# Attention ahead of a mixture of experts: all products of the exponentials with V in float32, in halves of 64 query columns

## The chip, the core and the metric

The kernel runs on one core of a Trainium2 chip. The metric is the time of one execution on the device, in microseconds (us). The core's engines work on their own queues, each in order, and wait for each other by semaphores: TensorE (PE in the profile, its weight loads PEld), VectorE (DVE), ScalarE (ACT), GpSimd (POOL) and SyncE (SP), which here issues DMAs, as ScalarE does.

## The reference

```python
def attention(q, k, v, g_q, g_k):            # 8 batches, 12 heads, 448 positions, 64 wide, float32
    q_n = q / sqrt(mean(q * q) + 1e-6) * g_q
    k_n = k / sqrt(mean(k * k) + 1e-6) * g_k
    scores = q_n @ k_n.T / sqrt(64)
    attn = exp(scores - max(scores))
    attn = attn / (sum(attn) + 1e-9)
    return attn @ v

x = attention(...)                           # 3584 tokens x 768
logits = x @ w_gate                          # 8 experts
# pairs (token, expert) in falling order of logits: a token goes to an expert if it has none
# yet and the expert has fewer than 448
out[mask_e] = maximum(x[mask_e] @ w1[e], 0) @ w2[e]
```

## The kernel before

The first part, the class `Attention`, takes about 470 us; `Router` and `Experts` take the rest. Attention works on 24 groups of four heads, two pairs of heads in a group. The 448 keys of two neighbouring heads make seven units of 128 keys: three full ones of the first head, unit 3 with 64 keys of either, and three of the second. The steps of a group:

- q and k are loaded, squared (ScalarE), summed (VectorE), scaled by their norms and g (GpSimd), split into a high and a low float16 half (ScalarE high, GpSimd low) and transposed by DMA. A first round of products gives row maxima (`max_score` on TensorE, `max_reduce` on VectorE), which go into q's operand as one more row.
- `scores` (lines 553 and 548) writes the scores of two units into PSUM (ring `psc`), keys in the partitions, and `exp` (line 564) makes of them one float32 tile `e`, 128 x 896, on ScalarE. A group has seven such tiles, d = 0 to 6, each of two units.
- `av` (lines 589 to 617) multiplies the exponentials, as the stationary operand, with V, 64 columns and a column of ones for the sum. For each pair of heads there are seven tasks w. Tasks 0 to 2 and 4 to 6 are whole blocks of 128 query columns of one head; each adds up four key units. Task 3 takes the last 64 columns of the first head into PSUM partitions 0 to 63 and the first 64 of the second into 64 to 127, and issues the two in turn.
- `x_norm`, `x_hi` and `x_lo` (lines 619 to 653) divide by the sums and split the result into float16 halves.

A product with V takes one of two forms, by the tile d. In a *wide* tile (`WIDE`) e is multiplied in float32 by a scaled float32 copy of V, `v32` (line 599). In any other tile the product is split (lines 604, 606 and 608): the upper 16 bits of e, read in place as bfloat16 (`ph`), times the high half of V; the same times V's low half; and the rest `pl` = e - `ph` in float16 times the high half. `split` (line 580) makes `pl` on GpSimd for the tiles of `LO_POOL` and on VectorE for the others. `v_hi` (line 477) and `v_lo` (line 481) make V's halves `vs` on ScalarE and VectorE, `v_full` (lines 486 and 488) makes `v32` on ScalarE. `MIX` gives each group its form: the first three groups have five wide tiles of seven ("5"), the next eighteen have four ("4": 0, 2, 4 and 6), the last three none ("0").

`plan` lists the tasks with their queue, a cost and what they depend on, and `ORDER` is a table of numbers that sets the order in which all tasks are issued. Each engine executes its own in that order. The table of the last batches ends with the router's first steps.

```python
if self.wide(d):
    nc.tensor.matmul(out, self.T["e", d][:, i, q0:q0 + m], self.v32[...], start=first, stop=last)
    continue
h, l = self.T["ph", d], self.T["pl", d]
nc.tensor.matmul(out, h[:, i, q0:q0 + m], vh, start=first, stop=False)
nc.tensor.matmul(out[:, :64], h[:, i, q0:q0 + m], vl[:, :64], start=False, stop=False)
nc.tensor.matmul(out, l[:, i, q0:q0 + m], vh, start=False, stop=last)
```

Of the kernel before, what the change touches and what calls it, by code (L numbers as in the profile page):

```python
# [89 lines left out]
class Attention:  # L90
# [21 lines left out]
    WIDE = {"5": (0, 2, 4, 6, 3), "4": (0, 2, 4, 6), "3": (0, 2, 4), "p": (0, 2, 4), "2": (2, 4), "0": ()}  # L112
    LO_POOL = {"5": (1, 5), "4": (1, 3, 5), "3": (1, 3, 5), "p": (1, 3, 5, 6), "2": (1, 3, 5), "0": (1, 3, 5)}
    MIX = "555" + 18 * "4" + "000"

    def __init__(self, ctx, tc, q, k, v, g_q, g_k, w_gate, xd, logits, router):
# [53 lines left out]
        def values(i):  # L170
            t, r = self.vs[i], self.vraw[i]
            G.memset(t[:, 0, :, 64:65], 1.0)
            for s in range(2):
                h = slice(64 - 64 * s, 128 - 64 * s)
                G.memset(t[h, 0, 2 * s + 1:8:4, 64:65], 0.0)
                G.memset(r[h, 4 * s + 3::8], 0.0)
            G.memset(self.v32[i][:, :, :, 64:65], 1.0)
# [22 lines left out]
        self.pl = {}  # L200
# [249 lines left out]
    def slot(self, a, u, s):  # L450

        w = self.block(a, u) % 4
        return 8 * (w < 2) + 2 * (2 * a + s) + w % 2
# [5 lines left out]
    def quads(self, t, n):  # L459
        return t.rearrange("p (x y) d -> p x y d", y=4)[:, :, 2 * n:2 * n + 2]  # L460

    def narrow(self, g):

        n = [d // 2 for d in (0, 2, 4, 6) if d not in self.by_group(self.WIDE, g)]
        return slice(n[0], n[-1] + 1, max(1, n[-1] - n[0]) if len(n) == 2 else 1) if n else None

    def halves_v(self, g):

        r, vs = self.vraw[g % 2], self.vs[g % 2].rearrange("p j (n x y) d -> p j n x y d", n=2, y=2)
        yield self.quads(r, 1), vs[:, 0, 0, :, :, :64], vs[:, 1, 0, :, :, :64]  # L470
        x = self.narrow(g)
        if x:
            yield self.quads(r, 0)[:, x], vs[:, 0, 1, x, :, :64], vs[:, 1, 1, x, :, :64]

    def v_hi(self, g):
        for r, h, l in self.halves_v(g):
            self.nc.scalar.activation(h, r, AF.Copy, scale=self.VS)

    def v_lo(self, g):
        for r, h, l in self.halves_v(g):  # L480
            self.nc.vector.scalar_tensor_tensor(l, r, self.VS, h, op0=OP.mult, op1=OP.subtract)
# [78 lines left out]
    def exp(self, d):  # L560
# [4 lines left out]
        self.T["ph", d] = e.bitcast(BF).rearrange("p i (c h) -> p i c h", h=2)[:, :, :, 1]  # L565

    def by_group(self, what, g):
        return what[self.MIX[g]]

    def pooled(self, d):  # L570
        g, n = divmod(d, 7)
        return n in self.by_group(self.LO_POOL, g)

    def wide(self, d):
        return d % 7 in self.by_group(self.WIDE, d // 7)

    def split(self, d):
# [5 lines left out]
    def av(self, n):  # L583
# [1428 lines left out]
```

## Time and profile before

| | |
|---|---|
| median of 3 runs | 964.99 us (964.6 to 966.69) |
| the profiled execution | 969.8 us |
| its span, first to last instruction | 968.0 us |
| TensorE busy | 908.1 us (94%), 9212 matmuls |
| VectorE, ScalarE, GpSimd busy | 666.8, 468.8, 437.8 us |
| attention's last products with V | 467 us |

The span is read in stretches: the first 50 us are a start in which TensorE is often without work, from 50 to about 400 the groups follow each other evenly, from 400 to 470 the last groups end without new loads, and behind 470 stand the router and the experts. A matmul's row has a modelled end, and rows overlap; what a matmul costs is read from the start of one to the start of the next. A row "x8" is eight instructions of one kind in a row, and its start is that of the first. A form such as 128*64 says how many rows and columns of the array a matmul uses.

### The profile page before, as it was taken

The numbers are of one execution on the slowest core, as the hardware profiler recorded it, in microseconds if no ns is written. First come the engines' busy times: TensorE is split into PE (matmuls) and PEld (weight loads), VectorE is DVE, ScalarE is ACT, GpSimd is POOL, SyncE is SP. The second block draws the span as 40 slices with busy tenths as digits, with TensorE's granted clock in tenths as the row PEclk, the third lists the DMA queues.
The fourth block names the chain that finished last, engine by engine and source line by source line (L and its number), as shares of the span: only waits on it lengthen the run. The fifth ranks groups of instructions, "written<-read, shape, count | busy, mean of one in ns | idle before, by whom it ended". The sixth has DMA issues, their size and how long they took to land.

```text
span 968.0 us, 22733 instructions
## 1 busy us (share of the span) xinstructions
PE 908.1 (94%) x9212; PEld 583.0 (60%) x9212; DVE 666.8 (69%) x1507; ACT 468.8 (48%) x732; POOL 437.8 (45%) x430
## 2 busy tenths in 40 slices
PE   2899999998999999999779999999999999999996
PEld 1467766666776667676655655556555565655553
DVE  6788896877678767998789777776775858234110
ACT  4867766665775756656324343434342414233110
POOL 7799989778798868853210202111202011120001
PEclk9899999999999989999789999999999999999999
DMA  6397999979999998976163938576766739482101
GB/s 166 100 171 172 197 206 184 205 199 201 219 207 206 188 214 176 172 173 129 60 208 119 265 136 252 181 233 192 216 185 214 202 131 309 156 189 105 34 17 41
DMA packets 278817, 167.76 MB, mean 173 GB/s; under 512 B 198806, under 2 KB 265878, under 8 KB 277688
## 3 DMA queue, kind: packets, MB, share of 16 engines
q1 hardware_dynamic: 254168, 139.43, 60.1%
q0 software_dynamic: 4704, 22.10, 7.0%
q10 hardware_dynamic: 19840, 4.79, 2.6%
q8 instruction: 72, 1.18, 0.5%
q14 instruction: 33, 0.27, 0.1%
HBM read 94.49 MB, written 22.02 MB: 120 GB/s over the span
## 4 chain that ended last, share of the span: by engine, by line
issue 33%; PE 7%; POOL 5%; DVE 2%; DMA 2%; SPq 1%; ACT 0%; POOLq 0%; DVEq 0%
PE ph L1775 6%; POOL rows L1708 2%; POOL out_dram L1811 2%; PE py L1792 1%; DMA stage<-in_moe_w_dram 1%; SPq L1713 1%; DMA xd<-xm 0%; PE rp L1350 0%; DMA rows<-xd,idx 0%; POOL spacer L1810 0%; DVE or L1325 0%; DVE cmp L1335 0%; DVE w1l L1695 0%; PE rp L1421 0%; ACT w2h L1691 0%
## 5 line engine op out<-in xcount | busy, mean ns | idle before, releaser
L1775 PE MATMUL ph<-xt,w1h 128*128 128x448 f16 (+2 forms) x804 | 209.7, 344 | 0.0
L564 ACT ACTIVATE e<-psc 128x896 f32<-128x896 f32 x168 | 152.3, 916 | 94.1 <-PE psc L553 53.3
L599 PE MATMUL po<-v,e 128*128 128x65 f32 (+1 forms) x1392 | 183.2, 269 | 0.6 <-DVE q L412 0.3
L599 PEld LDWEIGHTS po<-v,e 128*128 128x128 f32 (+1 forms) x1392 | 154.5, 179 | 22.3 <-issue 17.1
L1811 POOL DMA_INDIRECT out_dram<-y,idx x32 | 32.7, 1020 | 288.6 <-ACT y L1794 254.7
L580 POOL TENSOR_TENSOR pl<-e 128x896 f16<-128x896 f32 x69 | 118.1, 1713 | 65.9 <-ACT e L564 50.6
L553 PE MATMUL psc<-q,k 128*128 128x448 f16 x576 | 138.1, 361 | 9.6 <-ACT e L564 5.6
L1775 PE MATMUL ph<-xt,w1l 128*128 128x448 f16 (+2 forms) x402 | 135.1, 344 | 0.0
L530 DVE TENSOR_REDUCE mx<-pm 128x2 f32<-128x896 f32 x96 | 104.0, 1084 | 32.2 <-PE pm L519 28.8
L1792 PE MATMUL py<-w2h,hl 128*128 128x384 f16 x384 | 125.0, 326 | 0.0
L1792 PE MATMUL py<-w2h,hh 128*128 128x384 f16 x384 | 125.0, 326 | 0.0
L1792 PE MATMUL py<-w2l,hh 128*128 128x384 f16 x384 | 125.0, 326 | 0.0
L1775 PEld LDWEIGHTS <-w1h 128*128 128x128 f16 x804 | 74.0, 97 | 63.5 <-issue 1.9
L604 PE MATMUL po<-vs,e 128*128 128x65 f16 (+1 forms) x840 | 110.3, 196 | 0.4 <-DVE xm L653 0.4
L606 PE MATMUL po<-vs,e 128*128 128x64 f16 (+1 forms) x840 | 110.0, 194 | 0.0
L608 PE MATMUL po<-vs,pl 128*128 128x65 f16 (+1 forms) x840 | 109.3, 194 | 0.1
L1763 ACT ACTIVATE hh<-ph 128x448 f16<-128x448 f32 x64 | 34.8, 544 | 144.2 <-PE ph L1775 142.5
L1792 PEld LDWEIGHTS <-hh 128*128 128x128 f16 x768 | 73.2, 97 | 46.7
L604 PEld LDWEIGHTS <-e 128*128 128x128 bf16 (+1 forms) x840 | 87.3, 118 | 15.5 <-issue 9.6
L1765 DVE SCALAR_TENSOR_TENSOR hl<-ph,hh 128x448 f16<-128x448 f32 x64 | 39.4, 619 | 72.9 <-ACT hh L1763 72.9
L1708 POOL DMA_INDIRECT rows<-xd,idx x32 | 32.2, 1005 | 123.7 <-PE rp L1543 65.5
L1794 ACT ACTIVATE y<-py 128x384 f32<-128x384 f32 x48 | 23.6, 491 | 129.8 <-PE py L1792 97.0
(292 smaller groups left out, 1811.7 us busy)
## 6 DMA issues: line engine op xcount, KB each, us to landing
stage<-in_moe_w_dram SPq DMA_DIRECT2D x64, 768.0 KB
vraw<-in_v_dram SPq DMA_DIRECT2D x24, 384.0 KB
xd<-xb SPq DMA_DIRECT2D x8, 1152.0 KB
qkraw<-in_q_dram SPq DMA_DIRECT2D x23, 384.0 KB
qkraw<-in_k_dram SPq DMA_DIRECT2D x23, 384.0 KB
k<-k SPq DMA_DIRECT2D x44, 112.0 KB
q<-q SPq DMA_DIRECT2D x44, 112.0 KB
xd<-xm SPq DMA_DIRECT2D x16, 96.0 KB
```

What stands on the lines that cost most here:

```text
L530: self.nc.vector.tensor_reduce(m, p[:, :k, :448], axis=AX.X, op=OP.max)
L553: nc.tensor.matmul(p[:, i, :448], kt[:, a, n:n + 128], qt[:, a, 448 * s:448 * s + 448], start=st, stop=not st)
L564: self.nc.scalar.activation(e, p[:, :, :448], AF.Exp, scale=scale)
L580: eng.tensor_tensor(l, self.T["e", d], self.T["ph", d], op=OP.subtract)
L599: nc.tensor.matmul(out, self.T["e", d][:, i, q0:q0 + m], self.v32[g % 2][:, self.by_group(self.WIDE, g).index(d % 7), i, :], start=first, ...
L604: nc.tensor.matmul(out, h[:, i, q0:q0 + m], vh, start=first, stop=False)
L606: nc.tensor.matmul(out[:, :64], h[:, i, q0:q0 + m], vl[:, :64], start=False, stop=False)
L608: nc.tensor.matmul(out, l[:, i, q0:q0 + m], vh, start=False, stop=last)
L1708: nc.gpsimd.indirect_dma_start(out=g[:n, c, :], out_offset=None, in_=self.xd, in_offset=bass.IndirectOffsetOnAxis(ap=idx[:n, c:c + 1], axi ...
L1775: nc.tensor.matmul(p, a[:, i, c], x[:, b, o], start=j == 0, stop=j == 17)
L1792: nc.tensor.matmul(p, a[:, f, s], b[:, f, o], start=st, stop=sp)
L1811: st = nc.gpsimd.indirect_dma_start(out=self.out, out_offset=bass.IndirectOffsetOnAxis(ap=self.router.idx[k][:n, c:c + 1], axis=0), in_=y[ ...
```

## The change

All tiles are treated as wide, in all groups. The split products, `pl`, `vs`, `v_hi`, `v_lo` and `MIX` are gone. `v_full` makes one scaled float32 copy `v1` of a whole group's V on GpSimd, in one instruction. `av` treats each whole block as task 3 was treated: as two parts of 64 query columns, the first into PSUM partitions 0 to 63 and the second into 64 to 127, and issues them in turn.

```diff
-        self.vs = tiles(2, [128, 2, 16, 65], F16, "vs")
-        self.v32 = tiles(2, [128, max(map(len, self.WIDE.values())), 2, 65], F32, "v32")
+        self.v1 = tiles(2, [128, 16, 65], F32, "v1")
...
     def v_full(self, g):
-        r, o, wide = self.vraw[g % 2], self.v32[g % 2], [d for d in self.by_group(self.WIDE, g) if d != 3]
-        x = slice(wide[0] // 2, wide[-1] // 2 + 1)
-        self.nc.scalar.activation(o[:, :len(wide), :, :64], self.quads(r, 0)[:, x], AF.Copy, scale=self.VS)
-        if 3 in self.by_group(self.WIDE, g):
-            self.nc.scalar.activation(o[:, 4, :, :64], r[:, 6:14:4], AF.Copy, scale=self.VS)
+        self.nc.gpsimd.tensor_scalar(self.v1[g % 2][:, :, :64], self.vraw[g % 2], self.VS, None, op0=OP.mult)
...
-    def split(self, d):
-        l = self.T["pl", d] = self.w.tile([128, 2, 448], F16, name="pl", bufs=self.RINGS["pl"])
-        eng = self.nc.gpsimd if self.pooled(d) else self.nc.vector
-        eng.tensor_tensor(l, self.T["e", d], self.T["ph", d], op=OP.subtract)
...
-                if self.wide(d):
-                    nc.tensor.matmul(out, self.T["e", d][:, i, q0:q0 + m],
-                                     self.v32[g % 2][:, self.by_group(self.WIDE, g).index(d % 7), i, :], start=first, stop=last)
...
+                nc.tensor.matmul(out, self.T["e", d][:, i, q0:q0 + m], self.v1[g % 2][:, self.slot(a, u, s)],
+                                 start=u == us[0], stop=u == us[-1])
...
         if w == 3:
             parts = [part(po[:64, w], 0, 384, 64), part(po[64:, w], 1, 0, 64)]
-        elif w < 3:
-            parts = [part(po[:, w], 0, 128 * w, 128)]
         else:
-            parts = [part(po[:, w], 1, 64 + 128 * (w - 4), 128)]
+            s, q = (0, 128 * w) if w < 3 else (1, 64 + 128 * (w - 4))
+            parts = [part(po[64 * n:64 * n + 64, w], s, q + 64 * n, 64) for n in range(2)]
...
-            put("vhi", "A", "vhi", self.v_hi, g, after=[("v", g), *once("v", g)], make=("vh", g), opens=[("V", g)],
+            put("vfull", "P", "values", self.v_full, g, after=[("v", g), *once("v", g)], make=("V", g), opens=[("V", g)],
                 uses=[("vraw", g)])
...
     ORDER = (
-        "0o02060v0-0w030z000x050+09010A0410080B070y12141t130C151v0D0p0s1611170t181u1Q190u1S1A1R1w1T1x1P1G1U1y1V1H1B1q"
+        "0o02060v0-0w030z000x050+09010A0410080B070y12141r130C151t0D0p0s1611170t181s1Q190u1S1A1R1u1T1v1P1G1U1w1V1H1B1o"
```

The numbers in the new table are other ones since there are fewer tasks; the 2133 tasks that both kernels have stand in the same order in both.

On TensorE, in the middle of attention (group 11), a run of products with V between scores (L553, now L517) and maxima (L519, now L483). Before, from the end of a tile's scores on:

```order
L553 LDWEIGHTS k_3017
L553 MATMUL psc<-q_3065,k_3017 128x448
L553 LDWEIGHTS k_2_127
L553 MATMUL psc<-q_1_129,k_2_127 128x448
L604 LDWEIGHTS e
L604 MATMUL po<-vs_134,e 128x65
L606 LDWEIGHTS e
L606 MATMUL po<-vs_134,e 128x64
L608 LDWEIGHTS pl
L608 MATMUL po<-vs_134,pl 128x65
L599 MATMUL po<-v_0_138,e 128x65 x2
```

Now, at the same place:

```order
L517 LDWEIGHTS k_2856
L517 MATMUL psc<-q_2904,k_2856 128x448
L517 LDWEIGHTS k_2_127
L517 MATMUL psc<-q_1_129,k_2_127 128x448
L542 MATMUL po<-v_0_136,e 64x65 x32
L542 MATMUL po<-v_1_137,e 64x65 x8
L483 LDWEIGHTS q_3493
L483 MATMUL pm<-k_1_126,q_3493 128x448
```

The alternation of float16 and float32 products on 128 columns has become five blocks of eight float32 products on 64 columns; they now stand between products that use the full array and products that use half its rows.

On GpSimd, where V of group 10 is made (the operand v_0_136). Before, between the scaling of another group's k and q and the next group's square roots:

```order
L317 TENSOR_TENSOR kn<-qkraw,st 128x896
L342 TENSOR_TENSOR qn<-qn,gg 128x896
L580 TENSOR_TENSOR pl<-e 128x896 x2
L379 TENSOR_TENSOR ks_3421<-kn,ks_3421 128x2x7x64
L295 TENSOR_TENSOR st<-st 128x28
```

Now, at the same place:

```order
L310 TENSOR_TENSOR kn<-qkraw,st 128x896
L335 TENSOR_TENSOR qn<-qn,gg 128x896
L452 TENSOR_SCALAR v_0_136<-vraw_132 128x16x64
L372 TENSOR_TENSOR ks_3235<-kn,ks_3235 128x2x7x64
L288 TENSOR_TENSOR st<-st 128x28
```

The two differences are gone, and the copy of V stands there, at the place in the table that ScalarE's copy had.

## Rows read from the trace of the kernel before

**Rows 1.** Busy time of each engine in stretches of the span: start and end, length, busy us and instructions of TensorE, its weight loads, VectorE, ScalarE and GpSimd, the granted TensorE clock as a share of 2.4 GHz, the DMA engines' mean share, GB/s.

```profile
50.00:100.00 50.00, 47.99 (x543) 34.05 (x543) 42.60 (x64) 35.33 (x59) 46.25 (x40) 1.00 0.88 181
50.00:400.00 350.00, 334.06 (x4195) 241.16 (x4196) 275.71 (x428) 234.26 (x397) 294.69 (x241) 0.99 0.94 196
250.00:300.00 50.00, 49.15 (x632) 35.84 (x631) 38.37 (x59) 33.34 (x54) 44.29 (x40) 1.00 1.01 205
```

**Rows 2.** Who the matmuls waited for from 50 to 400 us: us in total, times, longest us.

```profile
PE psc L553 <- ACT e L564: 4.5, 4, 1.6
PE psc L553 <- DMA q<-mt: 3.7, 5, 2.1
PE pm L519 <- DMA k<-k: 2.7, 4, 1.2
PE po L712 <- DMA xt<-xb: 1.7, 1, 1.7
```

**Rows 3.** TensorE in order of time, a run of whole blocks in a group "4": start us, length us, engine, line, operation, tiles, form, count.

```profile
246.71 0.64 PE L599 MATMUL po<-v,e 128*128 128x65 f32 x4
247.18 0.19 PE L604 MATMUL po<-vs,e 128*128 128x65 f16 x1
...
247.36 0.64 PE L599 MATMUL po<-v,e 128*128 128x65 f32 x4
...
248.02 0.63 PE L599 MATMUL po<-v,e 128*128 128x65 f32 x4
```

**Rows 4.** TensorE in order of time, the start of two middle blocks.

```profile
112.27 0.40 PE L599 MATMUL po<-v,e 128*64 128x65 f32 x8
112.50 0.20 PE L604 MATMUL po<-vs,e 128*64 128x65 f16 x2
...
232.33 0.40 PE L599 MATMUL po<-v,e 128*64 128x65 f32 x8
232.57 0.20 PE L604 MATMUL po<-vs,e 128*64 128x65 f16 x2
```

**Rows 5.** Groups of TensorE's instructions with V by form: count, busy us, mean ns of one, idle before.

```profile
L599 PE MATMUL po<-v,e 128*128 128x65 f32 x1044 | 164.0, 282 | 0.6 <-DVE q L412 0.3 <-DVE xm L653 0.2
...
L604 PE MATMUL po<-vs,e 128*128 128x65 f16 x630 | 92.1, 195 | 0.4 <-DVE xm L653 0.4
```

**Rows 6.** TensorE in order of time, passages between forms: a product on 128*128, maxima on 64*128, scores on 128*128, a product on 128*128.

```profile
253.01 0.19 PE L608 MATMUL po<-vs,pl 128*128 128x65 f16 x1
253.13 0.36 PE L519 MATMUL pm<-k,q 64*128 64x448 f16 x2
253.33 0.35 PE L519 MATMUL psc<-k,q 64*128 64x448 f16 x2
253.62 0.93 PE L553 MATMUL psc<-q,k 128*128 128x448 f16 x4
254.38 0.56 PE L599 MATMUL po<-v,e 128*128 128x65 f32 x4
```

**Rows 7.** TensorE in order of time, a middle block behind maxima.

```profile
363.85 0.35 PE L519 MATMUL psc<-k,q 64*128 64x448 f16 x2
364.13 0.45 PE L599 MATMUL po<-v,e 128*64 128x65 f32 x8
364.41 0.20 PE L604 MATMUL po<-vs,e 128*64 128x65 f16 x2
```

**Rows 8.** Groups of GpSimd's instructions up to 480 us, by form.

```profile
L580 POOL TENSOR_TENSOR pl<-e 128x896 f16<-128x896 f32 x69 | 118.1, 1713 | 65.9 <-ACT e L564 50.6 <-PE po L608 12.6 <-DVE z L633 2.3
...
L317 POOL TENSOR_TENSOR kn<-qkraw,st 128x896 f32<-128x896 f32 x22 | 37.6, 1711 | 1.1
...
L159 POOL MEMSET q<- 64x448 f32 x2 | 0.9, 466 | 0.1
```

**Rows 9.** In order of time: the last product of group 8 on TensorE, the first read of group 10's raw V on ScalarE, GpSimd where V of group 10 is made now, and group 10's first product on TensorE.

```profile
213.75 0.19 PE L608 MATMUL po<-vs,pl 128*128 128x65 f16 x1
...
215.55 0.62 ACT L477 ACTIVATE vs<-vraw 128x512 f16<-128x512 f32 x1
...
221.43 2.10 POOL L342 TENSOR_TENSOR qn<-qn,gg 128x896 f32<-128x896 f32 x1
223.80 1.68 POOL L580 TENSOR_TENSOR pl<-e 128x896 f16<-128x896 f32 x1 [0.27 <-ACT e L564]
...
228.02 1.89 POOL L379 TENSOR_TENSOR ks<-kn,ks 128x896 f16<-128x896 f32 x1
...
228.89 0.64 PE L599 MATMUL po<-v,e 128*128 128x65 f32 x4
```

**Rows 10.** Groups of ScalarE's and VectorE's instructions that go, up to 480 us, by form.

```profile
L477 ACT ACTIVATE vs<-vraw 128x512 f16<-128x512 f32 x27 | 16.6, 626 | 1.6 <-DMA vraw<-in_v_dram 1.0 <-PE po L608 0.3 <-issue 0.2
...
L481 DVE SCALAR_TENSOR_TENSOR vs<-vraw,vs 128x512 f16<-128x512 f32 x27 | 27.5, 1027 | 0.0
...
L580 DVE TENSOR_TENSOR pl<-e 128x896 f16<-128x896 f32 x12 | 15.4, 1284 | 1.6 <-PE po L608 0.9 <-ACT e L564 0.8
```

**Rows 11.** Busy time in a stretch of the last groups, columns as in rows 1.

```profile
420.00:450.00 30.00, 28.06 (x474) 18.89 (x472) 29.44 (x47) 19.00 (x33) 10.50 (x6) 1.00 0.83 148
```

**Rows 12.** Who SyncE's transposes (L391) waited for from 50 to 400 us.

```profile
SPq L391 <- POOL st L298: 11.1, 5, 7.1
SPq L391 <- POOL qn L317: 10.7, 9, 3.0
```

More of the change, by code (lines that the diff above doesn't have):

```diff
@@ L594, in part @@
             for u in us:
-                vh, vl = (self.vs[g % 2][:, j, self.slot(a, u, s)] for j in range(2))
                 d, i = divmod(7 * pair + u, 2)
-                first, last = u == us[0], u == us[-1]
-                if self.wide(d):
-                    nc.tensor.matmul(out, self.T["e", d][:, i, q0:q0 + m],
-                                     self.v32[g % 2][:, self.by_group(self.WIDE, g).index(d % 7), i, :], start=first, stop=last)
-                    yield
-                    continue
-                h, l = self.T["ph", d], self.T["pl", d]
-                nc.tensor.matmul(out, h[:, i, q0:q0 + m], vh, start=first, stop=False)
-                yield
-                nc.tensor.matmul(out[:, :64], h[:, i, q0:q0 + m], vl[:, :64], start=False, stop=False)
-                yield
-                nc.tensor.matmul(out, l[:, i, q0:q0 + m], vh, start=False, stop=last)
+                nc.tensor.matmul(out, self.T["e", d][:, i, q0:q0 + m], self.v1[g % 2][:, self.slot(a, u, s)],
+                                 start=u == us[0], stop=u == us[-1])
                 yield
@@ L802, in put @@
             def put(name, queue, us, f, *args, **kw):
-                add(t + P[name], queue, US.get(us + queue, US.get(us)) + (whole if us in ("vhi", "vlo") else 0), f, *args, **kw)
+                add(t + P[name], queue, US.get(us + queue, US.get(us)), f, *args, **kw)
             for n in range(3):
@@ L870, in plan @@
                     make=("q2", *x), opens=() if a else [("q2", g)], uses=[("q2", g), ("mt", m)], move=(1.5 if a is None else 0.75, 0.1))
-            n = len([d for d in self.by_group(self.WIDE, g) if d != 3])
-            whole = 0.11 * (n < 4) + 0.12 * (4 - n)
-            put("vhi", "A", "vhi", self.v_hi, g, after=[("v", g), *once("v", g)], make=("vh", g), opens=[("V", g)],
+            put("vfull", "P", "values", self.v_full, g, after=[("v", g), *once("v", g)], make=("V", g), opens=[("V", g)],
                 uses=[("vraw", g)])
-            n = len(self.by_group(self.WIDE, g))
-            if n:
-                add(t + P["vfull"], self.engine("vfull", g), 0.14 + 0.115 * min(n, 4) + 0.25 * (n > 4), self.v_full, g, after=[("v", g), *once("v", g)], make=("V", g), opens=[("V", g)],
-                    uses=[("vraw", g)])
-            put("vlo", "D", "vlo", self.v_lo, g, after=[("vh", g)], make=("V", g),
-                uses=[("V", g), ("vraw", g)], port=True)
         two, turn = [], 0
@@ L901, in plan @@
                 two, turn = [], turn + 1
-        narrow = 0
-        assert len(self.MIX) == self.NG
         for d in range(nd):
@@ L912, in plan @@
                 frees=[("s", d)])
-            if not self.wide(d):
-                q = "P" if self.pooled(d) else "D"
-                add(d + P["split"], q, US["split" + q], self.split, d, after=[("e", d)], make=("e", d, 1),
-                    opens=[("pl", narrow)], uses=[("e", d)], port=True)
-                self.pl[d] = narrow
-                narrow += 1
         for n in range(2 * nd):
@@ L927, in plan @@
             ds = [(7 * pair + u) // 2 for u in us]
-            narrow = [d for d in ds if not self.wide(d)]
-            dt = US["wide"] * (len(ds) - len(narrow)) + US["narrow"] * len(narrow)
-            dt *= 0.55 if w == 3 else 1
-            add(n // 2 + self.LAG + P[f"av{n % 2}"] + P["av3"] * (w == 3), "T", dt, self.av, n, modes=[int(w == 3)] * 2,
-                after=[("V", g), *(("e", d) for d in set(ds)), *(("e", d, 1) for d in set(narrow))],
+            dt = US["wide"] * len(ds) * (0.5 if w == 3 else 1)
+            add(n // 2 + self.LAG + P[f"av{n % 2}"] + P["av3"] * (w == 3), "T", dt, self.av, n, modes=[1, 1],
+                after=[("V", g), *(("e", d) for d in set(ds))],
                 make=("po", pair), opens=[("av", pair)] if w == 0 else (), holds=[("po", ("po", pair))] if w == 0 else (),
-                uses=[("V", g), ("av", pair), *(("e", d) for d in set(ds)),
-                      *(("pl", self.pl[d]) for d in set(narrow))])
+                uses=[("V", g), ("av", pair), *(("e", d) for d in set(ds))])
         for pair in range(2 * self.NG):
```

128 lines of the change are left out of this document (47 added, 81 removed).

## The prediction

> **What bounds the kernel now.** The profiled execution has a span of 968.0 us and took 969.8; the median of the runs shown is 964.99, so 4.8 us below it. I make the sum against the 969.8 and take the 4.8 off at the end. First I read the stretches of the program with the busy time of each engine [rows 1]. Attention is over at about 470 us; nothing behind that is edited, so I let it move as a whole. In the 350 us from 50 to 400, TensorE is busy for 334.06, VectorE for 275.71, ScalarE for 234.26 and GpSimd for 294.69, and the DMA engines have a share of 0.94. TensorE is idle for 15.9 us of it. Since a busy matmul row is modelled, I checked who TensorE waits for [rows 2]: the four longest waits that name another engine or a DMA add up to 12.6 us for the matmul rows (exp 4.5, the row maxima 3.7, a copy of k 2.7, transposed x 1.7). So attention goes at TensorE's pace, some 95% of the time, and what a stage of attention is worth is what it takes of TensorE's issue time. That time is read as the step from one matmul's start to the next one's, not as the length of a row.
>
> **The products with V, by steps.** A block is 128 query columns of one head against four key units. In the 18 groups marked "4" it is two float32 units and two split ones. Three blocks that stand in a row begin at 246.71, 247.36 and 248.02 us [rows 3], so a block costs 0.655 us: four float32 issues take 0.47 (246.71 to 247.18; each float32 matmul is two issues in the trace, 0.11 to 0.12 apiece), and six float16 issues 0.03 each, 0.18. One float32 unit is thus 0.224 and one split unit 0.09.
>
> What the change puts there is already in the program: the middle block (w of 3) runs as two halves of 64 query columns, one in PSUM partitions 0 to 63 and one in 64 to 127. Eight float32 issues of that form begin at 112.27 and the next kind at 112.50, and again at 232.33 and 232.57 [rows 4]; the second of a pair starts at once. That is 0.23 to 0.24 us for eight issues, four half matmuls: I take 0.232, so 0.116 for a unit of 128 columns in halves, and 4 x 0.116 = 0.464 for a block.
>
> By stage, with 12 whole blocks and 2 middle ones in a group of four heads:
> - 18 groups "4": 216 blocks x (0.655 - 0.464) = 41.3 us less. A middle block has four split and four float32 halves; the eight float32 issues take 0.232 and the other twelve, side by side, 6 x 0.03 and a change of type, 0.44 in all, against 0.464 now: 36 x 0.02 = 0.8 more.
> - 3 groups "5": half of the blocks have three float32 units: 0.655 + 0.224 - 0.09 = 0.79. 3 x 6 x (0.191 + 0.326) = 9.3 less.
> - 3 groups "0", the last: all four units split, 12 x 0.03 = 0.36, against 0.464: 42 blocks x 0.104 = 4.3 more.
> Together 45.5 us less. The counts fit: 1044 float32 issues on 128 columns and 630 of each split kind [rows 5].
>
> **What it adds on TensorE.** All products with V now use half the array's columns; the scores use all of them, the maxima half the rows. Each passage between such forms costs a step more. From full columns into the maxima it is 253.01 to 253.13, 0.12 where 0.03 is usual; from the maxima into the scores 253.33 to 253.62, 0.29, where the pair before it took 0.20; from the scores into a float32 product of the same form, 253.62 to 254.38, it is 4 x 0.19, nothing more [rows 6]. So 0.09 a passage. In the instruction order I count 288 passages in attention before and 444 now: 156 x 0.09 = 14.0 us more. The first float32 pair behind a passage is slower as well: eight issues take 0.28 from 364.13 to 364.41 [rows 7], 0.05 over the 0.23. There are 181 runs of such products now; at 0.045 each 8.1 more. A block of today has its own such price (a change of type twice) in the 0.655.
>
> Sum on TensorE: -45.5 + 14.0 + 8.1 = **-23.4 us**.
>
> One price is not shown: leaving a float32 run in half columns for full columns or half rows. In the trace such a run is always followed by float16 in the same form. From below it is what other passages cost, 0.09, or less if only the second of two passages pays, against which two passages in a row stand that both pay [rows 6]; from above a whole matmul's length, 0.20, less the 0.03 step: 0.17. I take 0.09, since a float16 product of the same form leaves at that price, and the 0.17 goes into the range. The Trainium skill, "TensorEngine Tiling (Array Packing)", Tiling Modes, Key Properties, speaks against the change here: changing the tiling mode, not just the tile, drains TensorE. The trace agrees that there is a price and puts it at 0.09. An estimate from "TensorE: Matmul & The Clock Gate", Single matmul latency, for a lone matmul of 65 columns is 193 ns, 166 above its streaming time; with that for each of the 156 the sum would be -11.5.
>
> **What goes elsewhere.** GpSimd loses 69 differences at 1.713, 118.1 us, and gets 24 scaled copies of V, 128 x 1024 float32. The trace has no such operation: a GpSimd product of two inputs over 896 elements takes 1.711, which makes 1.96 for 1024; a memset over 448 takes 0.466, which makes 1.07 [rows 8]. I take 1.1, nearer to the row with fewer inputs, since this one reads a single tensor; 26 to 47 us for all, either way far less than what leaves.
>
> The copy adds a wait on GpSimd: for raw V, and for the last product of the group two before, whose V tile it overwrites. Behind it in GpSimd's queue stand the scaling and low halves of later k and q, and for those SyncE's transposes wait. Group 10 shows that both are over in time: the last product of group 8 is issued at 213.75, ScalarE reads group 10's raw V at 215.55, and the copy's place on GpSimd is behind a step that ends at 223.53 and ahead of one at 228.02; the first product of group 10 is due at about 228.9 [rows 9]. The two differences that stood between are gone, so even at 1.96 it is done by 225.5. I cost it at nothing; what hides it is GpSimd's own lighter queue. If that cover is gone, as it may be in the first 50 us, where group 0's second half waits on GpSimd, it is one copy, 1.1 to 2.0 us late. ScalarE and VectorE lose a high and a low half of V there, 0.6 and 1.0 [rows 10], which could give that back. I take 0, from -1.6 to +2.
>
> ScalarE loses the high halves, 16.6 us, and as many copies to float32 besides; VectorE the low halves and twelve differences, 27.5 + 15.4 [rows 10]. Neither is the bound from 50 to 400, so I count nothing for it: exp and maxima come no later, and their waits on TensorE I leave as they are. In the last groups VectorE is full, 29.44 us of 30 from 420 to 450, with TensorE at 28.06 [rows 11]. There VectorE's relief lets TensorE go at its own pace, which is 4.3 us slower by the third line above, and TensorE is late next. No DMA is added, and the table's order is the old one without the removed steps, so no other queue is passed.
>
> Against 969.8 this gives 946.4; less 4.8 for the median, **941.6 us**.
>
> **The rivals.**
> 1. *The DMA engines become the bound.* They move the same bytes in less time; the share is 0.94 over 50 to 400, and 1.01 is the most a stretch of 50 us shows [rows 1]. For: TensorE waits for row maxima and copies of k already [rows 2]. Against: SyncE's transposes wait for GpSimd's results, 11.1 and 10.7 us for two kinds of them alone [rows 12], and these now come earlier, so that transfers start sooner. At a ceiling of 0.97 the 350 us shrink to 0.94 x 350 / 0.97 = 339, 11 less, and the last groups give a little back: about 953.
> 2. *Leaving costs a drain.* 181 exits at 0.17 instead of 0.09 are 14.5 more: 956. By the skill's figure above, 953.
> 3. *TensorE's waits go too.* They come from exp and the k and q chains, and ScalarE and GpSimd are lighter. If all 15.9 vanish: 926.
> 4. *Waits take it all back*: TensorE, faster by 5%, waits for exp, the maxima and the copies of k where it hardly does now, and stays at 965.
> 5. *Slower: the halves don't run side by side.* In all pairs of the trace the two halves stream different V units against different exponentials. Now both stream the same V unit against neighbouring columns of one tile. If they took turns, 0.232 instead of 0.116 for each of 1344 pairs, it would be 156 us more: 1097. It decides from 0.133 a pair on; at 0.15 it is 987. Against: the scores' and results' halves also pair up. I know of no row that shows the same moving operand.
>
> **How the numbers follow.** Chances: forecast (932 to 948) 0.56; rival 1 0.15; rival 2 0.08; rival 3 0.10; rival 4 0.04; rival 5 and any like it 0.07. A difference of 0.2%, 2 us, is about what a measurement of this kernel can tell from none. Faster is then 0.89, same 0.04, slower 0.07. The range goes from the vanished waits to the dear exits, 927 to 957; rivals 4 and 5 and some of each end are left out.
>
> **What would show it.** Right: in the profile after, four pairs of float32 halves about 0.46 us apart, block after block; steps of 0.12 or so at passages; attention over at about 447 us; TensorE still busy for about 95% from 50 on; GpSimd's copies of V at 1 to 2 us, finished before the group's first product. Wrong: a DMA share at 1.0 with more TensorE waits for k, q and maxima (rival 1); long steps behind the last half of a run (rival 2); pairs of 0.2 (rival 5); a granted clock at its lower level, 1.2 GHz, in attention's middle. The row of the stretch [rows 1] has 0.99 of 2.4 GHz there, and 1.00 from 50 to 100, where the groups with the most float32 stand.

## The result and the profile after

The changed kernel takes **979.35 us** (median of four runs, 978.98 to 980.71); the kernel before, beside it, 965.84 (964.6 to 970.17). The ratio is 1.0141, with a 95% interval of 1.0112 to 1.0169. The forecast was 941.6 with a range of 927 to 957: it is wrong in sign, and the time lies outside the range. The profiled execution took 978.98 us with a span of 977.2, 9.2 more than the span before. Of these 8.2 are in attention: its last products begin at 475.3 us, against 467.1. (By the medians the loss is 13.5 us; the profiled execution of the kernel before, 969.8 us, was one of its longer ones, so a few us between two profiles are not sure.)

Busy time by stretch, columns as in [rows 1] and [rows 11], of the kernel after:

```profile
50.00:100.00 50.00, 43.21 (x729) 27.36 (x724) 40.49 (x61) 31.64 (x52) 43.61 (x38) 1.00 0.87 182
50.00:400.00 350.00, 312.21 (x5304) 199.54 (x5299) 245.37 (x402) 211.75 (x353) 249.57 (x205) 0.96 0.93 194
250.00:300.00 50.00, 44.99 (x811) 29.00 (x809) 33.08 (x54) 29.57 (x49) 38.83 (x34) 1.00 1.06 202
420.00:450.00 30.00, 28.66 (x515) 18.43 (x515) 20.56 (x35) 14.32 (x24) 9.28 (x4) 1.00 0.89 172
```

TensorE is busy for 312.21 of the 350 us, 21.9 less than before [rows 1]; its idle time went from 15.9 to 37.8, by the same 21.9. VectorE lost 30 us, ScalarE 23, GpSimd 45. One column stands where it was: the DMA engines' share, 0.93 against 0.94. Every engine got lighter, and attention got longer.

Who the matmuls wait for from 50 to 400 us, answering to [rows 2], of the kernel after:

```profile
PE psc L517 <- DMA q<-mt: 8.8, 6, 2.1
PE psc L517 <- ACT e L528: 7.6, 6, 2.1
PE pm L483 <- DMA k<-k: 6.6, 8, 1.9
PE pm L483 <- DVE mx L494: 6.5, 5, 3.0
PE psc L517 <- DMA q<-q: 3.0, 1, 3.0
```

The waits are longer, and none of the five stands before a product with V: scores wait for row maxima, for the exponentials and for q's second copy (`q<-q`), the maxima's products for k's second copy (`k<-k`) and for VectorE's reductions (`mx`).

TensorE in order of time, to set beside [rows 6], of the kernel after:

```profile
245.50 1.15 PE L542 MATMUL po<-v,e 128*64 128x65 f32 x32
246.59 0.93 PE L517 MATMUL psc<-q,k 128*128 128x448 f16 x4
...
251.63 1.57 PE L542 MATMUL po<-v,e 128*64 128x65 f32 x48
253.13 0.36 PE L483 MATMUL pm<-k,q 64*128 64x448 f16 x2
...
254.47 1.62 PE L542 MATMUL po<-v,e 128*64 128x65 f32 x48
256.02 0.36 PE L483 MATMUL pm<-k,q 64*128 64x448 f16 x2
```

Read by the starts: two blocks take 1.09 us (245.50 to 246.59), three take 1.50 and 1.55. The forecast's prices give 2 x 0.464 + 0.045 + 0.09 = 1.06 and 1.53. Over all 183 runs of such products in the trace (181 were counted in the order) the median is 0.619 us for 90 runs of one block, 1.085 for 47 of two, 1.552 for 26 of three, 0.02 to 0.03 above these prices. So the halves do stand side by side, and entry and exit cost what was taken.

GpSimd's copy of V and the low half of q that stands behind k's and q's steps, groups up to 480 us, of the kernel after:

```profile
L452 POOL TENSOR_SCALAR v<-vraw 128x1024 f32<-128x1024 f32 x24 | 66.5, 2770 | 17.9 <-PE psc L517 13.8 <-PE po L542 4.0
...
L377 POOL TENSOR_TENSOR qs<-qn,qs 128x896 f16<-128x896 f32 x22 | 41.7, 1897 | 52.2 <-ACT qs L345 48.5 <-DMA vraw<-in_v_dram 3.4 <-POOL tok L1026 0.4
```

The copy takes 2.77 us, above both bounds of the forecast (1.07 and 1.96).

Now the queue that the prediction looked at only for its waits. SyncE in order of time, start us, length us, line, operation, tiles, count, of the kernel before:

```profile
304.59 1.20 SPq L441 DMA_TRANSPOSE mt<-qm  x1
305.84 0.58 SPq L670 DMA_DIRECT2D xd<-xb  x1
308.82 1.55 SPq L448 DMA_DIRECT2D q<-mt  x2
310.41 0.60 SPq L226 DMA_DIRECT2D qkraw<-in_k_dram  x1
311.50 2.32 SPq L391 DMA_TRANSPOSE k<-ks  x1
313.93 1.07 SPq L226 DMA_DIRECT2D qkraw<-in_q_dram  x1
315.06 2.86 SPq L391 DMA_TRANSPOSE q<-qs  x1
317.97 1.23 SPq L361 DMA_DIRECT2D q<-q  x2
319.29 1.18 SPq L361 DMA_DIRECT2D k<-k  x2
```

and the same steps of the kernel after:

```profile
305.47 1.20 SPq L434 DMA_TRANSPOSE mt<-qm  x1
306.71 0.59 SPq L604 DMA_DIRECT2D xd<-xb  x1
310.73 1.56 SPq L441 DMA_DIRECT2D q<-mt  x2
312.33 0.44 SPq L219 DMA_DIRECT2D qkraw<-in_k_dram  x1
313.26 2.34 SPq L384 DMA_TRANSPOSE k<-ks  x1
315.72 1.93 SPq L219 DMA_DIRECT2D qkraw<-in_q_dram  x1
317.70 2.88 SPq L384 DMA_TRANSPOSE q<-qs  x1
320.63 1.22 SPq L354 DMA_DIRECT2D q<-q  x2
321.95 1.19 SPq L354 DMA_DIRECT2D k<-k  x2
```

SyncE issues one transfer behind the other: a transpose holds its queue for 1.2 to 2.9 us here, a second copy for 0.6. The lengths of all its records from 50 to 400 add up to 292.4 us before and 291.9 after. So a queue stood beside TensorE that was full for 84% of the stretch and waited, in order, for most of the rest; the page counts no DMA-issuing instruction as busy, so no engine's row shows it. The Trainium skill, "Perfetto Trace Analysis", What "DMA-bound" means, names such a queue as one of the forms: an issuing engine whose track is solid DMA slices. The trace has it solid for 84%; the run without V's loads below shows that this fill alone does not set the pace.

In the changed kernel the same step begins at 305.47 instead of 304.59, then the copies of the maxima (`q<-mt`) stand still for 3.4 us until their transpose has landed (307.30 to 310.73) instead of 2.4, and at `k<-k` the lag is 2.7 us. The starts of the groups say the same (a group has 32 score matmuls, so every 32nd begins one): group 2 at 78.4 us before and 77.4 after, group 8 at 179.9 and 179.5, group 15 at 311.1 and 311.3, group 20 at 404.3 and 408.5, the last products at 467.1 and 475.3. For two thirds of attention the pace is the old one although TensorE has less to do; then 4 us are lost before group 20 and 4 behind it, in this pair of profiles.

### The profile page after: what moved, and what is told of

Same layout as the page of the kernel before. It is cut to its first block, busy times and chain, and to the rows that moved or that the text cites. A ratio compares the mean times of both kernels' runs of the same rounds, so it can differ in the third digit from the quotient of the medians.

```text
span 977.2 us, 25519 instructions
## 1 busy us (share of the span) xinstructions
PE 896.2 (92%) x10674; PEld 544.8 (56%) x10676; DVE 620.3 (63%) x1468; ACT 443.3 (45%) x681; POOL 383.5 (39%) x383
## 4 chain that ended last, share of the span: by engine, by line
PE 26%; issue 15%; DVE 3%; DMA 2%; POOL 2%; SPq 2%; ACT 1%; POOLq 0%; DVEq 0%
PE ph L1687 14%; PE py L1704 8%; DMA stage<-in_moe_w_dram 2%; SPq L1625 2%; PE py L1713 1%; POOL out_dram L1723 1%; POOL rows L1620 1%; PE rp L1333 1%; PE py L1653 1%; PE rp L1262 0%; DMA rows<-xd,idx 0%; ACT w2h L1603 0%; DVE w1l L1607 0%; DVE or L1237 0%; DVE w2l L1607 0%
## 5 line engine op out<-in xcount | busy, mean ns | idle before, releaser
L542 PEld LDWEIGHTS po<-v,e 128*64 128x64 f32 x5376 | 178.7, 140 | 56.4 <-issue 49.8
L542 PE MATMUL po<-v,e 128*64 128x65 f32 x5376 | 199.9, 227 | 0.4 <-ACT e L528 0.2
L517 PE MATMUL psc<-q,k 128*128 128x448 f16 x576 | 141.0, 367 | 19.7 <-DMA q<-mt 8.8
L494 DVE TENSOR_REDUCE mx<-psc 128x2 f32<-128x896 f32 x74 | 78.1, 1058 | 8.1 <-PE psc L483 6.9
L517 PEld LDWEIGHTS <-k 128*128 128x128 f16 x576 | 46.7, 99 | 62.6 <-issue 26.8
L452 POOL TENSOR_SCALAR v<-vraw 128x1024 f32<-128x1024 f32 x24 | 66.5, 2770 | 17.9 <-PE psc L517 13.8
L1607 DVE SCALAR_TENSOR_TENSOR w2l<-stage,w2h 128x768 f16<-128x768 f32 x64 | 60.1, 951 | 13.7 <-ACT w2h L1603 13.7
L377 POOL TENSOR_TENSOR qs<-qn,qs 128x896 f16<-128x896 f32 (+1 forms) x25 | 44.8, 1794 | 52.8 <-ACT qs L345 49.0
```

Of the source, the lines that this page charges most:

```text
L377: self.tt("loq", g, a)(self.half(t, 64, a), self.paired(self.T["qn", g][:, self.of(a)], a), self.half(t, 0, a), op=OP.subtract)
L452: self.nc.gpsimd.tensor_scalar(self.v1[g % 2][:, :, :64], self.vraw[g % 2], self.VS, None, op0=OP.mult)
L494: self.nc.vector.tensor_reduce(m, p[:, :k, :448], axis=AX.X, op=OP.max)
L517: nc.tensor.matmul(p[:, i, :448], kt[:, a, n:n + 128], qt[:, a, 448 * s:448 * s + 448], start=st, stop=not st)
L1607: self.later(0.93, lambda w=w: self.nc.vector.scalar_tensor_tensor(l[:, w], v[:, w], self.WS, h[:, w], op0=OP.mult, op1=OP.subtract), k, i)
```

## The experiments

Three theories were set against each other from the start. A: GpSimd's copy of V, 2.77 us ahead of k and q in its queue, is what costs. B: the transfers, on the DMA engines and through SyncE's queue, pace the groups in both kernels, so that TensorE's relief turns into waits. C: TensorE's issue time was mis-priced. D came in for one run: the waits lower TensorE's clock, and that costs. Ratios are to the kernel before on the same chip, so two kernels are best compared by them; 0.001 is 1 us.

| kernel | median us | before | ratio | 95% interval |
|---|---|---|---|---|
| changed | 979.35 | 965.84 | 1.0141 | 1.0112-1.0169 |
| copy_scalar | 983.61 | 970.12 | 1.0135 | 1.008-1.0191 |
| copy_two_only | 985.54 | 970.12 | 1.0144 | 1.0102-1.0187 |
| light_after | 972.34 | 970.12 | 1.0017 | 0.998-1.0055 |
| light_before | 965.98 | 970.12 | 0.9951 | 0.9923-0.998 |
| filler | 985.37 | 967.27 | 1.0188 | 1.0106-1.027 |
| less_dma_before | 947.97 | 967.45 | 0.9779 | 0.9701-0.9856 |
| less_dma_after | 936.98 | 967.45 | 0.966 | 0.9584-0.9736 |
| no_v_load_before | 950.75 | 970.16 | 0.9789 | 0.9724-0.9854 |
| no_v_load_after | 962.75 | 970.16 | 0.9941 | 0.99-0.9981 |
| no_v_after | 965.99 | 969.73 | 0.9965 | 0.9923-1.0008 |
| split_last3 | 976.02 | 967.45 | 1.0095 | 1.0053-1.0137 |
| dup_after | 992.67 | 967.27 | 1.0274 | 1.0165-1.0383 |
| dup_before | 1015.76 | 967.27 | 1.0476 | 1.037-1.0583 |
| dup_split3 | 985.06 | 967.27 | 1.0192 | 1.0107-1.0277 |
| dupq_after | 973.38 | 970.16 | 1.0005 | 0.9973-1.0037 |
| dupq_before | 999.4 | 969.73 | 1.0296 | 1.0237-1.0355 |
| dupq_split3 | 969.95 | 970.16 | 0.9985 | 0.9944-1.0025 |
| dupq_split3_scalar | 967.21 | 969.73 | 0.998 | 0.9943-1.0017 |

### The copy of V: on ScalarE, and left out

```diff
-        self.nc.gpsimd.tensor_scalar(self.v1[g % 2][:, :, :64], self.vraw[g % 2], self.VS, None, op0=OP.mult)
+        self.nc.scalar.activation(self.v1[g % 2][:, :, :64], self.vraw[g % 2], AF.Copy, scale=self.VS)
...
-            put("vfull", "P", "values", self.v_full, g, after=[("v", g), *once("v", g)], make=("V", g), opens=[("V", g)],
+            put("vfull", "A", "values", self.v_full, g, after=[("v", g), *once("v", g)], make=("V", g), opens=[("V", g)],
```

> The changed kernel with V's scaled float32 copy made by ScalarE (one activation of 128 x 1024) instead of GpSimd, at the same place of the order. Theory A (the copy: 2.77 us each time, 66 us in all, ahead of later k and q in GpSimd's queue, is what costs): GpSimd is 66 us lighter, ScalarE about 26 us heavier with 140 us idle, and the time falls by 15 us or more, to 945-964. Theory B (the loads, transposes and small copies of the DMA queues pace the groups, whatever the engines do): no change beyond 4 us, 975-983. Theory C (TensorE's own issue time was mis-priced): no change either, 975-983.

```diff
+        if g < 2:
             self.nc.gpsimd.tensor_scalar(self.v1[g % 2][:, :, :64], self.vraw[g % 2], self.VS, None, op0=OP.mult)
```

> The changed kernel with the copy of V made for groups 0 and 1 only; the products of later groups read those two again (left out: 22 copies). Theory A (the copy costs): as without it at all, 940-960. Theory B (the DMA queues pace the groups): 975-983, since all loads and transposes stay. Theory C (TensorE's issue time): 975-983.

Ratios of 1.0135 and 1.0144 against 1.0141: with the copy elsewhere, or with 22 of 24 copies gone, nothing changes. GpSimd's busy time from 50 to 400 falls to 198 and 201 us, and nobody uses it. Theory A falls. It falls although the copy does hold something up. Who SyncE's transposes of the changed kernel waited for, from 50 to 400 us:

```profile
SPq L384 <- POOL v L452: 8.9, 5, 2.2
```

These 8.9 us do not come back as time when the copies go (in the kernel before, 11.1 us of such waits were for the differences, `pl`): a wait in a trace is not yet a cost.

In the run without the copies the profile's chain of waits reaches back through attention. Its shares by line from 100 to 400 us:

```profile
by line: PE po L543 12.3%; PE psc L518 11.2%; DMA mt<-qm 7.3%; DMA q<-qs 6.2%; DMA q<-mt 5.2%; issue 4.6%; ACT e L529 3.7%; DMA qkraw<-in_k_dram 3.3%; DMA q<-q 3.3%; DMA k<-k 3.2%; SPq L219 2.7%; DMA vraw<-in_v_dram 2.5%; PE psc L513 2.4%; 
```

TensorE's three lines are 26%, and the seven lines of DMAs 31%. Had TensorE alone been the bound, it would be nearly all.

### TensorE's work taken away and added

```diff
-            for u in us:
+            for u in (us[0], *us[2:]):
```

> The changed kernel with one of the four key units left out of every block's products with V (the second of each; the exponentials are still made). At the step seen in the trace, 0.116 us a unit of 128 columns, TensorE has 336 x 0.116 = 39 us less. Theory C (TensorE's issue time bounds attention): some 35-39 us less, 940-945. Theory B (the DMA queues pace the groups): only the last groups, where nothing is loaded any more, gain, some 5 us: 970-977. Theory A (GpSimd's copy): 970-979 as well, since the copy stays.

> The kernel before with the same unit left out of every block. By the steps of the prediction a unit is 0.224 us in float32 and 0.09 split, 0.157 on the mean, so TensorE has about 50 us less. If TensorE alone bounded attention, as the prediction had it: 915-925. If the DMA queues stood close behind it (theory B): a gain of 20 us at most, 945-965, and the starts of groups 2 to 15 hardly move. Theory A says nothing of this kernel, since GpSimd makes no copy in it, and goes with 915-925.

Busy time from 50 to 400 us, of the kernel before without that unit:

```profile
50.00:400.00 350.00, 301.14 (x3577) 199.41 (x3575) 276.09 (x431) 232.90 (x396) 294.12 (x241) 0.93 0.92 197
```

The old kernel with about 50 us less of products is at 0.9951: 5 us faster. Its group 16 begins at 326.4 us, where it began at 328.0. The clock took a part of the 50 us back (51.2 us at 1.2 GHz from 50 to 400, against 10.2). Even so TensorE is busy for 32.9 us less and idle for 48.9 instead of 15.9. This run answers the forecast's first step: TensorE alone did not set the pace even before. In the changed kernel 39 us less give 12 (1.0141 to 1.0017), 5.8 of them from group 21 on (44.2 us to the last products, against 50.0). The other 6 come earlier, so its TensorE has some say there too, if far from all.

```diff
-            for u in us:
+            for u in us if a else (us[0], us[1], *us[1:]):
```

> The changed kernel with more work on TensorE, none else: the second key unit of every block of the first half of each group is multiplied twice (its share counts double in the output). 168 x 0.116 = 19.5 us more on TensorE, which brings it to about the busy time of the kernel before. Theory B (the DMA queues pace the groups): the time stays within 5 us of the changed kernel, 975-985, except for some 2 us in the last groups. Theory C (TensorE's issue time): 19 us more, 995-1000. Theory D (the stalls lower TensorE's clock, 27.3 us at 1.2 GHz against 17 before, and that is what costs): with fewer stalls the clock stays up and the time falls, 968-976.

19.5 us more on TensorE cost some 5 (1.0188, with overlapping intervals). Theory C would have 19, theory D a gain. Of D this is a weak test, since the time at 1.2 GHz between 50 and 475 us only fell from 27.3 to 20.5. Two kernels with the same products say more: copy_scalar has 41.0 us at 1.2 GHz in that stretch and copy_two_only 23.9, and their ratios are 1.0135 and 1.0144. So the clock is not the main cause; a small part is not excluded.

### Transfers taken away

Without V's loads from group 2 on:

```diff
     def load_v(self, g, n):
+        if g > 1:
+            return
```

> The changed kernel without V's loads from group 2 on (the first two groups' V stays in the tiles and is copied again): 448 KB less a group, some 28 us of 16 engines' time from 50 to 400, and no step of the chain from k and q to the row maxima. If the DMA engines' time paces the groups: 950-965. If the chain's steps do, by their latency: 972-980. If GpSimd's copy is late because raw V lands late: 965-975.

> The kernel before without V's loads from group 2 on. If the DMA engines' time paces the groups, it gains what TensorE's idle time (15.9 us) allows and less than the changed kernel: 953-962. If the chain's steps do: 962-968.

Without the second copies of k and q from group 3 on as well:

```diff
+            if g > 2:
+                continue
             e = self.engine("dup" + name[0], g)
             if e == "S":
                 self.nc.sync.dma_start(o, i)
```

> The kernel before with less to transfer: V's loads are left out from group 2 on and SyncE's second copies of k and q from group 3 on (what they would bring stays as the first groups left it), some 50 us of 16 engines' time out of about 330 in the 350 us. TensorE's work is the same. Theory B (the DMA queues pace the groups, TensorE stands close behind): TensorE's 334 of 350 us let attention shrink by its idle time and little more, 8 to 16 us: 950-960. If TensorE alone bounds: 962-968, no change but a wait or two. If neither, but the chain of steps from load to row maxima by its latency: 955-965.

> The changed kernel with the same transfers left out. Theory B: the pacing queues are relieved, TensorE's lighter products become worth what the prediction gave them (-23 us, with +4 in the last groups among it), and the time falls below the relieved kernel before: 930-942, at least 12 us under it. If the products' prices were wrong (theory C), it stays above the relieved kernel before: 960-975. If GpSimd's copy is what is late (theory A), 970-979.

Busy time from 50 to 400 us, columns as above. The kernel before without V's loads:

```profile
50.00:400.00 350.00, 343.73 (x4434) 251.46 (x4433) 290.93 (x459) 243.90 (x413) 309.09 (x249) 1.00 0.87 182
```

The kernel before without V's loads and second copies:

```profile
50.00:400.00 350.00, 346.91 (x4484) 253.70 (x4484) 294.41 (x467) 246.50 (x418) 311.20 (x252) 1.00 0.78 157
```

The changed kernel without both:

```profile
50.00:400.00 350.00, 337.31 (x6036) 219.71 (x6031) 276.18 (x460) 231.55 (x388) 270.20 (x218) 1.00 0.82 160
```

V's loads are no step on the way from k and q to the maxima, though they stand in the same queue of SyncE, and no product waits for V in either trace. Yet without them both kernels gain about 20 us, four times what 50 us of products gave. In the kernel before the last products begin at 446.8 us instead of 467.1, with TensorE's work unchanged. (The packets' time, all durations up to 480 us divided by 16, falls from about 405 us to 366.) Transfers pace the groups: theory B. SyncE's records still fill 288 of the 350 us there, against 292, so it is not the queue's fill that changed. The DMA engines' share fell from 0.94 to 0.87, and the transposes of k and q hold the queue for 1.7 us at the median instead of 2.3 and 2.2, so that more of them pass in the same time. The kernel before then stops at TensorE, busy for 344 to 347 of 350 us at the full clock, and the second copies give it nothing more (0.9789, 0.9779). Only there, with the transfers out of the way, is TensorE the bound that the forecast took it for, and only there the change pays: the changed kernel is at 0.966, 11 us under it (936.98 against 947.97), where the forecast had 23.4 and the expectation at least 12.

But without V's loads alone the changed kernel is still 12 us slower than the old one, with 23 us of TensorE's time idle. Who the matmuls of the changed kernel without V's loads wait for from 50 to 400:

```profile
PE pm L485 <- DMA k<-k: 9.1, 9, 2.6
PE pm L485 <- DVE mx L496: 3.4, 5, 1.9
```

The maxima wait for k's second copy. Whether GpSimd's copies of V delay k there was the next question; V's loads and copies were both left out, by the two edits above together:

> The changed kernel without V's loads and without the copies of V from group 2 on. If GpSimd's copies delay k and q once the transfers are lighter: 10 us or more under the run without the loads alone (962.75), 940-952. If the copies are hidden there too: 959-966.

0.9965 against 0.9941: they do not. The wait for `k<-k` is 9.1 us with them and 7.4 without, and the time is no shorter.

### The last three groups

Groups 21 to 23 as before, with V's halves and the differences, and 0 to 20 as changed:

```diff
-    MIX = "555" + 18 * "4" + "000"
+    MIX = "hhhhhhhhhhhhhhhhhhhhh000"
...
-        elif w < 3:
+        elif self.wide(7 * g):
+            s, q = (0, 128 * w) if w < 3 else (1, 64 + 128 * (w - 4))
+            parts = [part(po[64 * n:64 * n + 64, w], s, q + 64 * n, 64) for n in range(2)]
+        elif w < 3:
             parts = [part(po[:, w], 0, 128 * w, 128)]
```

> The changed kernel with the last three groups as in the kernel before (all units split into float16 halves on 128 query columns, V's halves by ScalarE and VectorE); groups 0 to 20 as changed. By the steps the float32 halves cost these groups 42 x 0.104 = 4.3 us, and from the start of group 20 to the last product the trace has 66.8 us after against 62.8 before. Theory B: 4 us come back, 973-977, and the other 4 to 6 us of the loss, between groups 15 and 20, stay. If the loss is elsewhere: 978-981.

In this text `h` is a group with all units in float32. The ratio is 1.0095 against 1.0141: 4.4 us come back, where the forecast's term was 4.3. The intervals overlap, so the size is not sure, but the place agrees: from group 21's first scores to the last products it is 50.0 us in the changed kernel (425.3 to 475.3), 46.8 with the split units (423.3 to 470.1) and 47.0 in the kernel before (420.1 to 467.1).

### Transfers moved to other engines

The second copies on VectorE (k) and ScalarE (q); nothing is left out:

```diff
-    ENG = dict(lok="P", loq="P", dupk="S", dupq="S", normk="P", normq="P", gain="P", vfull="A", root="P")
+    ENG = dict(lok="P", loq="P", dupk="D", dupq="A", normk="P", normq="P", gain="P", vfull="A", root="P")
```

> The changed kernel with the second copies of k and q (112 KB a piece, four a group) made by VectorE (k) and ScalarE (q) instead of SyncE's DMAs, at the same places of the order. This takes some 32 of 300 us of 16 DMA engines' time and leaves every result as it is. Theory B: the changed kernel gains 10-20 us, 958-970. If the copies' wait for the transposes stops VectorE and ScalarE, which exp and maxima queue behind: 980-1000. Theories A and C: 975-983.

> The kernel before with the same edit. Theory B with TensorE close behind: it gains less than the changed kernel does, 0-12 us: 953-967; its TensorE was idle for 15.9 us only, and its VectorE and ScalarE have less room.

> The changed kernel with the last three groups split as before and the second copies of k and q on VectorE and ScalarE. Theory B: 4 us under the run with those copies alone, 954-966, at or under the kernel before; otherwise as there.

All three are slower than without the edit, clear of the intervals only in the kernel before (1.0476), and the gains expected of dup_before and dup_split3 are missed. The DMA share of the changed kernel falls from 0.93 to 0.81, but TensorE's wait for exp doubles from 7.6 to 14.6 us. For dup_after the second of the expectations holds: copies that wait for a transpose (VectorE's of k, 5.6 us in all), or take 1.007 us each, stop the exponentials and maxima queued behind them. A relief that costs a fuller queue elsewhere is none.

With q's second copy alone on VectorE, far behind its transpose, in the changed kernel, in the kernel before, with the split last groups, and with V's copy on ScalarE as well:

```diff
-    ENG = dict(lok="P", loq="P", dupk="S", dupq="S", normk="P", normq="P", gain="P", vfull="A", root="P")
+    ENG = dict(lok="P", loq="P", dupk="S", dupq="D", normk="P", normq="P", gain="P", vfull="A", root="P")
```

> The changed kernel with the second copy of q alone made by VectorE (two copies of 64 x 896 float16 a group, 1.007 us each in the run with both copies moved: 44 us on VectorE, which was idle for 105 of 350). It stands 20 to 100 steps behind its transpose, so VectorE should not wait for it. The results are kept; the DMA engines have some 20 us less. If their time paces the groups: 965-973. If VectorE's row maxima come late by it: 980-990.

> The kernel before with the second copy of q alone made by VectorE (some 20 us less of the DMA engines, 40 us more on VectorE, which has 276 of 350). If the transfers pace the groups in it as well: 4-8 us less, 960-964. If VectorE, fuller here than in the changed kernel, becomes late: 968-980.

> The same with the last three groups split as in the kernel before. If the DMA engines' time paces the groups: 3 to 4 us under the run with that copy alone, 960-970, beside the kernel before at 965-968.

> The changed kernel with the last three groups split, q's second copy on VectorE and the copy of V on ScalarE. If GpSimd's copies cost something once transfers are lighter: 4 us or more under the same with the copy on GpSimd (969.95), 960-966. If not: 966-974.

The changed kernel gains 13 us (1.0141 to 1.0005), with the split last groups 15 (0.9985), and with V's copy on ScalarE 16 (0.998). None of the three differs from the kernel before by more than its interval, so no version is shown to beat it. In the kernel before the same edit costs 3%, more than either expectation. Who its matmuls wait for from 50 to 400:

```profile
PE po L599 <- DVE xm L653: 10.3, 8, 2.7
PE pm L519 <- DVE mx L530: 3.9, 5, 1.8
```

VectorE, which still makes low halves of V and differences there, is now late with the results that free PSUM. So the change's relief, costed at nothing, has a worth: it is the room that a transfer can be moved into. That it is VectorE's relief is read from these waits; no run gives that back alone.

## Why the prediction was wrong

**The step that failed is the first**, "attention goes at TensorE's pace, some 95% of the time, and what a stage of attention is worth is what it takes of TensorE's issue time". It was read from a busy share (334.06 of 350) and from short waits. Both also fit a pipeline in which TensorE and the transfers are each nearly full, and the share of 0.94 stood in the same row [rows 1]. light_before shows that the share was no bound: 50 us of products less are worth 5. no_v_load_before shows what was: with all products in place and V's loads gone, attention ends 20 us earlier. That TensorE waits for nobody for long says little either, since an engine that has just enough work to cover a pace set elsewhere waits as little.

**The prices were right.** Halves at 0.464 a block, an entry at 0.045, an exit at 0.09: within 0.03 a run. TensorE's busy time in the 350 us fell by 21.9. Leaving costs no drain beyond that, so rival 2 falls, and rival 5 with it, since the halves do not take turns.

**Rival 1 came nearest to the cause, with the wrong size.** "The DMA engines become the bound" was priced from a ceiling of 0.97, 11 us better than before. The share did not rise at all, 0.94 to 0.93: a share below 1 was taken for room. One reason may be that the transfers are issued in one order through one queue, 292 us of 350 in both kernels, and wait in it for each other and for the engines. That is argued; no run shows it by itself. What happened is rival 4, "waits take it all back", to which the forecast gave 0.04; rival 3, that the waits vanish, is its opposite.

**The last groups** cost 4.3 us in the forecast and 3.0 to 4.0 in the trace (50.0 us against 47.0 from the start of group 21 to the last products, 66.8 against 62.8 from that of group 20); split_last3 gives 4.4 back. There few loads are left and TensorE sets the pace of the changed kernel (28.66 of 30 us busy, and 5.8 us come back in light_after), so this term stood while its counterweight did not. That makes 3 to 4 of the 13.5 us.

**GpSimd's copy** was sized at 1.1 us, between 1.07 and 1.96, and measured 2.77. That it costs nothing was right all the same: copy_scalar, copy_two_only, no_v_after and dupq_split3_scalar, with it moved or gone, show no gain. SyncE's transposes did wait for it, but no longer than they had waited for the differences. ScalarE's and VectorE's relief shows no worth either, as forecast, as long as the transfers stay where they are.

**What stays open.** Last groups apart, the changed kernel is 0.95% slower than the old one (split_last3), in the profile 4 us between groups 15 and 20. The runs show what it is not: not the copy of V, not V's loads (the gap of 12 us is the same without them), and for the most part not TensorE's work (39 us less of it give 6 before the last groups). It goes when both kernels lose the second copies of k and q as well, and the changed kernel closes it when q's second copy leaves SyncE. So it most likely lies on the way from the transposes through SyncE's queue to the maxima, where waits for `mt<-qm` on SyncE grew from 16.6 to 21.2 us and those for `k<-k` on TensorE from 2.7 to 6.6. Why these come later in a kernel whose engines all have less to do was not settled. Nor is a part of the clock excluded: between the starts of groups 15 and 20 it was at 1.2 GHz for 13.6 us after and 6.8 before. Against it, between groups 2 and 8 it was so for 10.2 us after and not at all before, and only 0.6 us were lost there (102.1 against 101.5). That the order was written for other durations is a guess, which no run tests. Nor do the runs tell the DMA engines' time from SyncE's issue time: each edit that took transfers away took their issues as well (V's 24 loads are 13 us of SyncE's records). That SyncE's fill hardly changed in no_v_load_before while the share fell speaks for the DMA engines' time, but does not show it.

## What to carry to other kernels

A busy share of 95% does not make an engine the bound: look for every resource that is nearly full in the same stretch, and add up the issuing queue's own records, which count nowhere as busy here. None of these shares is a proof, the queue's neither. The cheapest proof is a kernel with some of the supposed bound's work left out; if the time hardly moves, price nothing by that engine's issue time. Relief is worth something only where it can be spent: here it paid after transfers had gone (11 us) or as room for one of them (13 us), and where loads are over the dearer form costs in full.

## What the runs showed of the hardware

- GpSimd's product of one float32 tensor with a constant, 128 x 1024, takes 2.77 us, 2.7 ns an element and partition. Its product of two tensors over 896 takes 1.687 in the same trace, 1.9 ns. The form with fewer inputs is the slower one here; its output has rows of 64 in steps of 65.
- SyncE's transpose of 128 x 1792 float16 holds its queue for 2.1 to 2.3 us at the median from 50 to 400 us before and after, up to 3.9, and for 1.7 us in no_v_load_before, where there is less to transfer.
- TensorE's clock fell more often where it was idle for longer, but not in every kernel. From 50 to 400 us it was at 1.2 GHz for 10.2 us in the kernel before (15.9 idle), 27.3 after (37.8 idle), 51.2 in light_before (48.9 idle), and never in less_dma_before (3.1 idle). But in dupq_before it was so for 68.3 us with 25.2 idle, and in copy_scalar for 38.6 with 37.0 idle, against 23.9 with 38.3 idle in copy_two_only.
- VectorE's copy of k, 64 x 896 float16 from one half of the partitions to the other, takes 1.007 us, 1.1 ns an element.
